# Two fetched tiles a block, copies as products with ones, and row stores on SyncE

## The chip, the cores and the metric

The kernel runs on one core of a Trainium2 chip. The metric is device time in microseconds (us), the median of three runs; the profile comes from one further execution. TensorE (PE in the profile, PEld for its weight loads), VectorE (DVE), ScalarE (ACT) and GpSimd (POOL) compute; SyncE (SP) issues transfers.

## The reference

A graph of 10000 nodes with 160000 random directed edges is propagated seven times, and a small attention runs over each node's eight states:

```python
h = x                                   # (10000, 128)
toks = [x]
for _ in range(7):
    msg = h[src] * deg_inv_sqrt[src, None] * deg_inv_sqrt[dst, None]
    h = segment_sum(msg, dst, N)        # one hop
    toks.append(h)
tok = stack(toks, axis=1)               # (N, 8, 128)
t = layernorm(tok)
attn = softmax((t @ wq) @ (t @ wk).T / sqrt(128))
o = tok + (attn @ (t @ wv)) @ wo
alpha = softmax(layernorm(o) @ w_r)
out = sum(alpha * o)                    # over the 8 tokens
```

## The kernel before

**Tables and slots.** The nodes lie in 79 tiles of 128. A hop keeps its input as a table in SBUF, `tab` (128 partitions, 79 tiles, 256 columns of f16: a high half and a low half of each value), and as rows in DRAM: `tabd` holds all tiles, `tabh` only the last ones. A *block* is the work for one tile of 128 destination nodes, some 2000 edges. Its edges are sorted by source into cells of 32 places (`CAP`). Four cells, for four source tiles, make one *slot tile* of 128 places. `NG` = 18 slot tiles cover the first 72 source tiles and are *gathered* from SBUF by TensorE: for each cell a matmul of 128 rows by 32 columns picks up to 32 rows of a source tile (line 578), four of them side by side fill one slot tile in PSUM. The 7 source tiles that remain are cut into 4 cells that make up `NI` = 1 slot tile, which is *fetched* from `tabh` by an indirect DMA that POOL issues (`fetch`, line 524). Edges beyond 32 in a cell go to one more tile, fetched from `tabd` (the index `i == NI`, matrix `Sov`). `NJ` = `NG` + `NI` is 19.

**A block** (`block`). Nine calls of `gather` fill nine PSUM banks in turn (ring of six), each with two slot tiles; each bank is copied to an f16 buffer `eb` of a ring (line 581; 14 buffers in hops 2 to 7), five of the nine by ACT and four by DVE (`evac`: ACT for 0, 2, 4, 5, 7). Then `begin` multiplies the fetched tiles into the accumulator (line 540), and `scat` multiplies each buffer by its 128 x 128 matrix of zeros and ones into it (line 554). The scatter of the last two buffers of a block is kept back (`lag` = 2) and runs behind the next block's gather. `close` sums the two halves (DVE, line 569).

**Behind it** stands `fin`: `entries` writes the next hop's table tile (ACT line 610, then DVE lines 611 and 612), `rows` stores it to DRAM (line 159, and line 163 for the tiles that `tabh` holds) and `token_out` scales the sum on POOL (line 619) and stores it as a token (line 621, SP). The last hop has `token_out` alone.

**Fetches.** `ahead` issues the fetches for the block two further on; the first of them is preceded by a copy of one column on POOL (line 523) that reads the block's first gather buffer, so that the fetch isn't issued too early. Fetches from `tabd` carry no such copy. Fetch tiles have three buffers. At a hop's start the overflow tiles of blocks 0 and 1 (`ogl`) can only be fetched when the last rows of the hop before have landed; line 567 uses them at these blocks' end.

**Stages.** Pass A and `decode` sort the edges. Hop 1 also makes the matrices of each block (`place`, `matrices`; lines 509 and 512 write them on DVE) and stores them in `GSd`. Hops 2 to 7 load them back (line 746, on SP, five buffers) and run the blocks in the order of tiles `4 * NG` to 78, then 0 to `4 * NG - 1`. The attention stage follows. The order on each engine comes from a scheduler that follows the order of the program where it can; every engine works its own list in order. Transfers that SP, ACT or POOL issue stand in that engine's list and wait there for their data.

Of the kernel before, what the change touches and what calls it, by code (L numbers as in the profile page):

```python
# [7 lines left out]
F32 = mybir.dt.float32  # L8
# [5 lines left out]
ALU = mybir.AluOpType  # L14
# [3 lines left out]

N, E, D, K = 10000, 160000, 128, 7
NT = 79  # L20
NG = 18
NI = 1
CELL = 334
NK = 79
NR = 10240
NCOL = E // 128
# [2 lines left out]
CAP = 32  # L29
NJ = NG + NI  # L30
NS = 4 * NJ
# [8 lines left out]
class Hops:  # L40
    def __init__(self, ctx, dp, missing, tab, tc, x, src, dst, dis):
# [31 lines left out]
                V.tensor_scalar(self.triw[:, w, :], ci, rf, None, op0=ALU.is_gt)  # L73
        self.ones32 = cp.tile([1, 128], F32, name="ones32")
        V.memset(self.ones32, 1.0)
        self.ones16 = cp.tile([128, 1], F16, name="ones16")
        V.memset(self.ones16, 1.0)
        self.iof = cp.tile([128, 128], F32, name="iof")
# [449 lines left out]
    def block(self, t, w, tab, og, pend, lag, runs, first, evac, fin, lead=False, late=False, mid=None, ahead=None,  # L528
              after=None):

        nc, V, A, T, G = self.nc, self.nc.vector, self.nc.scalar, self.nc.tensor, self.nc.gpsimd
        m = 257 if first else 256
        acc = []


        def fetched(i, start=False, stop=False):
            W = w[:, (NG + i) * 128:(NG + i + 1) * 128] if i < NI else self.Sov[:, t, :]
            T.matmul(acc[0][:, :256], W, og[i], start=start, stop=stop)  # L540
            if first:
                T.matmul(acc[0][:, 256:257], W, self.ones16, start=False, stop=False)

        def begin():
            acc.append(self.pacc.tile([128, 512], F32, name="acc", tag="acc"))
            for i in range(NI if late else NI + 1):
                fetched(i, start=i == 0)

        def scat(e, jj):
            if not acc:  # L550
                acc.append(self.pacc.tile([128, 512], F32, name="acc", tag="acc"))
            for j in range(e.shape[1]):
                J = 2 * jj + j
                T.matmul(acc[0][:, :m], w[:, J * 128:(J + 1) * 128], e[:, j, :m], start=first and J == 0,  # L554
                         stop=J == NG - 1 and not (first or late))
                if first and J == 0 and not lead:
                    for i in range(NI):
                        fetched(i)

        def close():  # L560
            if first:
                if lead:
                    for i in range(NI):
                        fetched(i)
                T.matmul(acc[0][:, 256:257], self.Sov[:, t, :], self.ones16, start=False, stop=False)
            if first or late:
                T.matmul(acc[0][:, :256], self.Sov[:, t, :], og[NI], start=False, stop=True)  # L567
            s = self.fp.tile([128, 128], F32, name="s")
            V.tensor_reduce(s, acc[0][:, 0:256].rearrange("p (h d) -> p d h", h=2), axis=X, op=ALU.add)  # L569
            fin(t, s, acc[0])  # L570

        def gather(jj):
            n = min(2, NG - 2 * jj)
            p = self.pg.tile([128, 2, 2, 128], F32, name="p")
            for j in range(n):
                for q in range(4):
                    s = 4 * (2 * jj + j) + q
                    T.matmul(p[32 * q:32 * q + 32, j], w[:, NJ * 128 + s * CAP:NJ * 128 + (s + 1) * CAP], tab[:, s, :], start=True, stop=True)  # L578
            e = self.ebuf[self.eb_i % len(self.ebuf)]
            self.eb_i += 1  # L580
            (A.copy if evac(jj) else V.tensor_copy)(e[:, :n, 0:256], p[:, :n].rearrange("p j h d -> p j (h d)"))  # L581
            pend.append(lambda: scat(e[:, :n], jj))

        jj = 0
        for i, n in enumerate(runs):
            for _ in range(n):
                gather(jj)
                if jj == 0 and not first and not mid:
                    ahead(self.ebuf[(self.eb_i - 1) % len(self.ebuf)][:, 0, 0:1])
                jj += 1  # L590
            if mid:
                mid(0)
            if not first:
                begin()
                if mid:
                    ahead()
            while len(pend) > lag:
                pend.pop(0)()
            if mid:
                mid(1)  # L600
            if after:
                after()
            if i == len(runs) - 1:
                pend.append(close)
            yield
# [17 lines left out]
    def run(self, ctx, att, nhop=K):  # L623
# [68 lines left out]
        with ExitStack() as c:  # L692
            self.gsp = c.enter_context(tc.tile_pool(name="gs2", bufs=5))
            self.pg = c.enter_context(tc.tile_pool(name="pg2", bufs=6, space=PSUM))
            self.pacc = c.enter_context(tc.tile_pool(name="pc2", bufs=2, space=PSUM))
            self.ogp = c.enter_context(tc.tile_pool(name="og2", bufs=3))
            self.fp = c.enter_context(tc.tile_pool(name="fp2", bufs=4))
            self.sp = c.enter_context(tc.tile_pool(name="sp2", bufs=2))
            self.more_ebufs(c.enter_context(tc.tile_pool(name="eb2", bufs=1)), 9, False)
            pend = []  # L700
            for k in range(2, nhop + 1):
                i = 1 - k % 2
                tab, din = self.tab[i], (self.tabd[i], self.tabh[i])
                ct = self.ctok[i]
                last = k == nhop
                V.tensor_scalar(ct, self.disT, self.sinv, None, op0=ALU.mult)


                def scale(part, n, i=i, k=k):
                    if part == 0 and n == 0 and k == 2:  # L710
                        self.count()
                    if part != 1 - n:
                        return
                    if n == 0:
                        mc = self.sp.tile([128, 1], F32, name="mc")
                        V.tensor_reduce(mc, self.mx[i], axis=X, op=ALU.max)
                        scale.m = self.colmax(self.pg, self.sp, mc, "p")
                        V.tensor_mul(scale.m, scale.m, self.rho)
                    else:
                        q = self.pow2_of(self.pg, self.sp, scale.m, 2.0 ** 8, "p")  # L720
                        V.tensor_mul(self.sinv, self.sinv, q[:, 1:2])
                        V.tensor_scalar(self.c1[i], self.dis2, q[:, 0:1], None, op0=ALU.mult)

                def fin(t, s, acc, k=k, ct=ct, last=last, i=i):
                    if not last:
                        self.entries(t, s, i)
                        self.rows(1 - i, self.tab[1 - i], t, t + 1, nc.scalar)
                    self.token_out(k, t, s, ct)


                order = [*range(4 * NG, NT), *range(4 * NG)]
                og = [[None] * (NI + 1) for _ in order]


                def ahead(n, after=None, og=og, order=order, din=din):
                    if n + 2 < NT:
                        for j in range(NI):
                            og[n + 2][j] = self.fetch(order[n + 2], j, din, after=None if j else after)
                    for m in range(0 if n == 0 else n + 2, min(n + 3, NT) if n >= 0 else 0):
                        og[m][NI] = self.fetch(order[m], NI, din, "ogl" if m < 2 else None)  # L740

                ahead(-2)
                ahead(-1)
                for n, t in enumerate(order):
                    w = self.gsp.tile([128, (NJ + NG) * 128], F8, name="w")
                    nc.sync.dma_start(w, self.GSd[t])
                    if k == 2 and n == 20:
                        att.constants(c, self.pg.tile([128, 512], F32, name="aw", tag="p"), self.ident)
                    if last and 40 <= n < 40 + 8 * FIRST:
                        att.load((n - 40) // 8, (n % 8,))  # L750

                    after = pend.pop() if n == 1 else None
                    for _ in self.block(t, w, tab, og[n], pend, 2, (9,), False, lambda jj: jj in (0, 2, 4, 5, 7), fin, n == 0, n < 2,
                                        (lambda part, n=n: scale(part, n)) if n < 2 and not last else None,
                                        lambda after=None, n=n: ahead(n, after), after):
                        pass
                while pend:
                    pend.pop(0)()
# [533 lines left out]
```

## Time and profile before

| | us |
|---|---|
| median of three runs (4150.82 to 4153.82) | 4152.88 |
| span of the profiled execution, first to last instruction | 4139.7 |
| TensorE busy | 3818.7 |
| VectorE busy | 3355.8 |
| ScalarE busy | 2692.1 |
| GpSimd busy | 1769.2 |

Busy time is that of the span; issuing a transfer and waiting for a semaphore count as idle. Hop 1 lies at about 410 to 1190 us, hops 2 to 7 from there to 3459, the attention stage behind. A row of the timeline gives start, duration, engine, line, operation, output and inputs, the number of instructions merged into it, and in brackets the idle time of the engine just before and what ended it. ACTq and SPq are the instructions of the queue that issue transfers.

### The profile page before, as it was taken

The page shows a single profiled execution, that of the slowest core. Times are in us where ns is not written, and L with a number is a line of the kernel's source. Part 1 is how long each engine was busy: PE and PEld are TensorE (multiplying, and loading weights), DVE is VectorE, ACT ScalarE, POOL GpSimd, SP SyncE. Part 2 cuts the span into 40 slices and gives each one's busy share as a digit, 9 for nine tenths or more (in the row PEclk, how much of TensorE's full clock was granted, in tenths as well). Part 3 has the DMA queues.
Part 4 walks back from the last instruction along what each step waited for, and adds up shares of the span by engine and source line. Part 5 has one row for each costly group of instructions (what it writes and reads, how often), then busy time and mean ns, then how long its engine had stood idle before and what let it go on. Part 6 is the DMA issues. An engine that isn't in the chain of part 4 may idle for free. (4 is left out here: it accounts for less than half of the span.)

```text
span 4139.7 us, 164058 instructions
## 1 busy us (share of the span) xinstructions
PE 3818.7 (92%) x69690; PEld 3021.9 (73%) x69690; DVE 3355.8 (81%) x6960; ACT 2692.1 (65%) x6830; POOL 1769.2 (43%) x2342
## 2 busy tenths in 40 slices
PE   5886889999989999999999999999999999999997
PEld 4665666666657777777777777777777887788785
DVE  8998999999967777777677777777775665999998
ACT  6883456666656665666566566656665657888885
POOL 0000333343345555555555555555555663222222
PEclk8998999999999999999999999999999999999998
DMA  3000444554556665665566656656666653222220
GB/s 109 23 2 17 143 148 153 152 157 150 158 163 185 186 184 180 185 185 184 179 184 186 181 183 186 186 176 186 187 185 191 188 184 105 75 72 81 72 77 17
DMA packets 321181, 594.87 MB, mean 144 GB/s; under 512 B 56183, under 2 KB 214101, under 8 KB 315189
## 3 DMA queue, kind: packets, MB, share of 16 engines
q1 hardware_dynamic: 220565, 478.42, 37.0%
q0 software_dynamic: 35392, 72.55, 6.4%
q10 hardware_dynamic: 64480, 33.33, 2.8%
q8 instruction: 546, 8.95, 0.9%
q14 instruction: 198, 1.62, 0.1%
HBM read 455.43 MB, written 128.67 MB: 141 GB/s over the span
## 5 line engine op out<-in xcount | busy, mean ns | idle before, releaser
L581 ACT CAST eb<-p 128x512 f16<-128x512 f32 x3065 | 1591.8, 600 | 670.9 <-PE p L578 575.6
L581 DVE CAST eb<-p 128x512 f16<-128x512 f32 x1912 | 1263.9, 688 | 439.1 <-PE acc L554 271.6
L578 PE MATMUL p<-tab,w 128*32 128x256 f16 x39816 | 1371.3, 275 | 105.0 <-ACT eb L581 38.1
L578 PEld LDWEIGHTS <-w 128*32 128x32 fp8e4 x39816 | 999.0, 96 | 406.7 <-issue 349.4
L554 PE MATMUL acc<-eb,w 128*128 128x256 f16 (+1 forms) x9954 | 1247.3, 274 | 9.2 <-ACT eb L581 2.3
L554 PEld LDWEIGHTS <-w 128*128 128x128 fp8e4 x9954 | 953.8, 98 | 172.7 <-issue 57.4
L524 POOL DMA_INDIRECT og<-tabh,oidx x553 | 616.6, 1115 | 769.2 <-DVE vi L476 389.0
L524 POOL DMA_INDIRECT og<-tabd,oidx x541 | 584.0, 1080 | 599.9 <-PE acc L554 262.7
L610 ACT ACTIVATE tab<-s,c 128x128 f16<-128x128 f32 x395 | 158.7, 402 | 359.7 <-DVE eb L581 262.9
L619 POOL TENSOR_SCALAR r<-s,ctok 128x128 f32<-128x128 f32 x474 | 295.7, 624 | 45.3 <-DVE s L569 28.2
L611 DVE SCALAR_TENSOR_TENSOR tab<-s,c,tab 128x128 f16<-128x128 f32 x395 | 139.0, 352 | 182.8 <-issue 166.5
L523 POOL COPY og<-eb 128x1 f16<-128x1 f16 x452 | 84.0, 186 | 422.7 <-ACT eb L581 422.7
L569 DVE TENSOR_REDUCE s<-acc 128x128 f32<-128x256 f32 x553 | 228.9, 414 | 23.1 <-PE acc L567 10.1
L991 ACT ACTIVATE junk<-tab 128x128 f32<-128x128 f32 x625 | 245.2, 394 | 0.0
L338 ACT ACTIVATE rs<-iof,rb 128x128 fp8e4<-128x128 f32 x784 | 231.9, 393 | 0.3
L512 DVE TENSOR_TENSOR w<-dsl,iof 128x2432 fp8e4<-128x2432 f16 x79 | 211.6, 2678 | 0.0
L977 PEld LDWEIGHTS po<-v,pT 128*128 128x128 f32 x1250 | 159.3, 193 | 43.6 <-issue 27.8
L966 PE MATMUL pv<-Wv,xT 128*128 128x131 f32 x1250 | 175.9, 283 | 2.5 <-ACT xT L946 1.5
L1049 POOL TENSOR_TENSOR p<-e,in 128x512 f32<-128x512 f32 (+1 forms) x40 | 40.8, 1021 | 320.7 <-DVE e L1047 320.7
L977 PE MATMUL po<-v,pT 128*128 128x128 f32 x1250 | 166.9, 277 | 7.0 <-DVE tab L983 5.4
L966 PEld LDWEIGHTS pv<-Wv,xT 128*128 128x128 f32 x1250 | 152.9, 191 | 19.3 <-issue 8.3
L540 PE MATMUL acc<-og,w 128*128 128x256 f16 x553 | 156.6, 283 | 0.0
(284 smaller groups left out, 4598.7 us busy)
## 6 DMA issues: line engine op xcount, KB each, us to landing
w<-gsd SPq DMA_DIRECT2D x474, 592.0 KB
gsd<-w SPq DMA_DIRECT2D x79, 592.0 KB
rb<-srow SPq DMA_DIRECT2D x79, 576.0 KB
tok<-r SPq DMA_DIRECT2D x546, 64.0 KB
tab<-tok SPq DMA_DIRECT2D x273, 128.0 KB
tabd<-tab ACTq DMA_DIRECT2D x395, 64.0 KB
og<-tabh,oidx POOLq DMA_INDIRECT x553
og<-tabd,oidx POOLq DMA_INDIRECT x541
```

The lines of the kernel that those rows point to most:

```text
L338: A.activation(ro[:, j - a, i, :], self.iof, AF.Abs_reciprocal_sqrt, scale=2.0 ** 21, bias=rb[:, j - VP, i:i + 1], saturate=False)
L512: V.tensor_tensor(w[:, :NJ * 128].rearrange("p (j d) -> p j d", d=128), dsl[:, g, :, None].to_broadcast([128, NJ, 128]), self.iof1[:, None ...
L524: self.nc.gpsimd.indirect_dma_start(out=o, out_offset=None, in_=src[0] if i == NI else src[1], in_offset=bass.IndirectOffsetOnAxis(ap=self ...
L554: T.matmul(acc[0][:, :m], w[:, J * 128:(J + 1) * 128], e[:, j, :m], start=first and J == 0, stop=J == NG - 1 and not (first or late))
L569: V.tensor_reduce(s, acc[0][:, 0:256].rearrange("p (h d) -> p d h", h=2), axis=X, op=ALU.add)
L578: T.matmul(p[32 * q:32 * q + 32, j], w[:, NJ * 128 + s * CAP:NJ * 128 + (s + 1) * CAP], tab[:, s, :], start=True, stop=True)
L581: (A.copy if evac(jj) else V.tensor_copy)(e[:, :n, 0:256], p[:, :n].rearrange("p j h d -> p j (h d)"))
L610: self.nc.scalar.activation(new[:, t, 0:128], s, AF.Copy, scale=c)
L619: self.nc.gpsimd.tensor_scalar(r, s, ct[:, t:t + 1], None, op0=ALU.mult)
L966: T.matmul(p[:, g - a, :], S[i]["xT"][:, g, :], Wv, start=True, stop=True)
L977: T.matmul(p[:, g - a, :], PT[i % 2][:, g, :], S[i]["v"][:, g, :128], start=True, stop=True)
L991: A.activation(j, S[i]["x"][:, g, :], AF.Square, bias=S[i]["x"][:, g, 0:1], scale=-1.0, accum_out=S[i]["sq"][:, g:g + 1])
```

## The change

`NG` becomes 17 and `NI` 2. The gather covers 68 source tiles; the remaining 11 are cut into 8 cells (`CELL` sets their width), which make two slot tiles, both fetched from `tabh`. `NJ` stays 19. The ninth call of `gather` then has one slot tile. Each block has two fetches from `tabh` and one from `tabd`; only the first carries the copy on POOL. `tabh` has 11 tiles, and a hop's order starts with those 11. DVE's copies of line 581 become products of the PSUM bank with a column of ones, broadcast over the bank. In hops 2 to 6 `rows` is issued by SP and not by ACT.

```diff
-NG = 18
-NI = 1
-CELL = 334
+NG = 17
+NI = 2
+CELL = 404
...
+        self.one = cp.tile([128, 1], F32, name="one")
+        V.memset(self.one, 1.0)
...
-            (A.copy if evac(jj) else V.tensor_copy)(e[:, :n, 0:256], p[:, :n].rearrange("p j h d -> p j (h d)"))
+            pv = p[:, :n].rearrange("p j h d -> p j (h d)")
+            if evac(jj):
+                A.copy(e[:, :n, 0:256], pv)
+            else:
+                V.tensor_tensor(e[:, :n, 0:256], pv, self.one[:, :, None].to_broadcast([128, n, 256]), op=ALU.mult)
...
-                        self.rows(1 - i, self.tab[1 - i], t, t + 1, nc.scalar)
+                        self.rows(1 - i, self.tab[1 - i], t, t + 1, nc.sync)
```

## The prediction

> **What bounds the kernel now.** I read four views in this order: busy time by stage, one block of a middle hop on each engine, the same block in the last hop, and the rows around a hop's start. First the stages (columns: busy us in 100 us with the number of instructions, granted clock, DMA share, GB/s).
>
> ```profile
> core 0: us, PE busy (x) PEld busy (x) DVE busy (x) ACT busy (x) POOL busy (x), PEclk, DMA share, GB/s
> 600.00:700.00 100.00, 91.48 (x1618) 67.48 (x1616) 98.01 (x136) 61.14 (x134) 38.09 (x22) 0.98 0.52 160
> 2400.00:2500.00 100.00, 97.18 (x1943) 77.97 (x1936) 74.59 (x148) 62.36 (x128) 58.84 (x85) 1.00 0.61 186
> 3200.00:3300.00 100.00, 100.00 (x2112) 84.92 (x2100) 66.88 (x115) 60.72 (x115) 63.43 (x92) 1.00 0.60 187
> ```
>
> The first row lies in hop 1: VectorE is at 98%. The second lies in hop 5, one of hops 2 to 6, the third in hop 7: TensorE is at 97 and 100% with the clock at 1.00. A block has 92 matmuls (72 of the gather, 2 of fetched tiles, 18 of the scatter), so 1943 in 100 us is 21 blocks, 2112 is 23. The same matmuls go 9% faster in hop 7, where no table entry is made. What hops 2 to 6 lose is seen in one block on PE, then on ACT:
>
> ```profile
> 2411.98 2.51 PE L578 MATMUL p<-tab,w 128*32 128x256 f16 x72
> ...
> 2414.66 2.13 PE L554 MATMUL acc<-eb,w 128*128 128x256 f16 x18
> 2416.72 1.49 PE L578 MATMUL p<-tab,w 128*32 128x256 f16 x48
> ```
>
> ```profile
> 2411.76 0.40 ACT L610 ACTIVATE tab<-s,c 128x128 f16<-128x128 f32 x1 [0.98 <-DVE eb L581]
> 2412.58 0.35 ACTq L159 DMA_DIRECT2D tabd<-tab  x1
> 2412.97 2.54 ACT L581 CAST eb<-p 128x512 f16<-128x512 f32 x5 [0.81 <-PE p L578]
> ```
>
> and the block of hop 7, PE and ACT:
>
> ```profile
> 3300.08 2.15 PE L578 MATMUL p<-tab,w 128*32 128x256 f16 x72
> ...
> 3304.45 2.15 PE L578 MATMUL p<-tab,w 128*32 128x256 f16 x72
> ```
>
> ```profile
> 3300.59 2.05 ACT L581 CAST eb<-p 128x512 f16<-128x512 f32 x4 [1.26 <-PE p L578]
> ```
>
> A block takes 2416.72 - 2411.98 = 4.74 us in hops 2 to 6 and 3304.45 - 3300.08 = 4.37 in hop 7. The gather itself takes 2.51 against 2.15. In hop 7 ACT empties the first PSUM bank 0.51 us after the gather began; in hop 5, 0.99 after (2412.97 - 2411.98). Between, ACT's own queue stands at the row store of line 159, which must wait for VectorE's half of the entry and then takes 0.35 to issue. After 48 matmuls all six gather banks are full and PE waits for that first copy. The view names "PE p" as releaser of ACT; its row of the queue shows the store.
>
> **Part 1, one slot tile fewer in the gather, one fetched tile more.** On PE this takes 4 gather matmuls (which run side by side) and one scatter matmul away and adds one fetched matmul: one step out of 38. A step is (2.13 - 0.27) / 17 = 0.11 us by the scatter row. So PE alone would need 4.37 - 0.11 = 4.26 us a block. On POOL it adds an indirect fetch per block, and POOL does them one at a time. A hop's start shows its pace with nothing to wait for, and a block behind it that of a fetch from the small table:
>
> ```profile
> 1966.22 0.94 POOL L524 DMA_INDIRECT og<-tabd,oidx  x1 [0.30 <-issue]
> 1967.47 0.95 POOL L524 DMA_INDIRECT og<-tabd,oidx  x1 [0.30 <-issue]
> 1968.72 0.95 POOL L524 DMA_INDIRECT og<-tabd,oidx  x1 [0.30 <-issue]
> 1969.70 0.62 POOL L619 TENSOR_SCALAR r<-s,ctok 128x128 f32<-128x128 f32 x1
> 1970.27 0.19 POOL L523 COPY og<-eb 128x1 f16<-128x1 f16 x1
> 1970.73 1.02 POOL L524 DMA_INDIRECT og<-tabh,oidx  x1 [0.27 <-issue]
> ...
> 1977.25 0.19 POOL L523 COPY og<-eb 128x1 f16<-128x1 f16 x1 [1.71 <-ACT eb L581]
> 1977.94 1.02 POOL L524 DMA_INDIRECT og<-tabh,oidx  x1 [0.51 <-POOL og L523]
> 1979.26 0.96 POOL L524 DMA_INDIRECT og<-tabd,oidx  x1 [0.30 <-PE acc L554]
> ```
>
> Start to start: copy to fetch 0.46, small-table fetch to the next fetch 1.32, big-table fetch to the token product 0.98, product to the next copy 0.57. POOL's turn without waits is 0.46 + 1.32 + 0.98 + 0.57 = 3.33 us now, far under 4.74. With a second small-table fetch it is 3.33 + 1.32 = 4.65 us. That is over PE's 4.26: the bound of hops 2 to 7 passes from PE to POOL, hidden as the fetches are today. POOL should then not wait at all: its copy needs ACT's first copy of the block, its fetches need fetched matmuls of earlier blocks, its product needs a sum of the block before, and PE is ahead in all of these. PE waits instead, for fetched tiles and, through the ring of 14 gather buffers (POOL's copy reads one of them, and it is written again in the next block), for POOL's copy. PE can get about one and a third blocks ahead, 5.5 us by estimate (4.26 plus the part of the next block up to the sixth buffer), before it is held; a hop keeps this head start once.
>
> The price of the added fetch is not shown in steady state. Below: spacing as between big-table fetches, 1.25 (1966.22 to 1967.47) for both small ones, so 4.65 - 0.14 = 4.51. Above: copy to fetch as at 1977.25, 0.69 instead of 0.46, so 4.88. I take 4.65, made of the rows nearest to a turn without waits. A gain below 4.26 is excluded, since PE stands there.
>
> **Part 2, rows stored by SP.** Both stores of `rows` leave ACT's queue. A block that also stores to the small table shows what an issue on ACT costs:
>
> ```profile
> 1989.98 1.49 PE L578 MATMUL p<-tab,w 128*32 128x256 f16 x48
> 1992.11 0.89 PE L578 MATMUL p<-tab,w 128*32 128x256 f16 x24 [0.64 <-ACT eb L581]
> ...
> 1995.21 1.49 PE L578 MATMUL p<-tab,w 128*32 128x256 f16 x48
> ```
>
> That block takes 1995.21 - 1989.98 = 5.23 us, 0.49 over 4.74 for one more store. So with the stores gone ACT starts as in hop 7 and PE's 4.26 holds in hops 2 to 6 too; the small table grows from 7 to 11 tiles, whose second store SP takes. The Trainium skill (DMA: Bandwidth & Descriptors, "Issuing engines are not separate DMA queues") says the issuing engine only matters for the time to initiate, usually small beside the transfer; the 0.49 us differ from that here, and by that rule blocks with two stores would stay at 5.23 - 0.11 = 5.12, eleven a hop over POOL's 4.65, and the sum would be 11 x 0.47 x 5 = 26 us smaller, 4128.
>
> On SP the stores stand behind the matrix load and the previous token store, which waits for POOL's product. With POOL a block late that delays rows and later matrix loads by about a block; five buffers hold the loads, and rows are read a hop later. Only the last rows of a hop are urgent. I price SP at 2 us a hop (0 to 4, by estimate: up to a block's wait at the hop's end). The transfers themselves (a matrix smaller by one tile of 37, one more fetch of 128 rows) fall on DMA engines that are at 0.61: 0.
>
> **Part 3, products with ones.** 4 of 9 PSUM copies in hops 2 to 7, and 16 in hop 1 (1912 - 4 x 474), become products with one PSUM and one broadcast SBUF operand; the ninth is half as large.
>
> ```profile
> L581 DVE CAST eb<-p 128x512 f16<-128x512 f32 x1912 | 1263.9, 688 | 439.1 <-PE acc L554 271.6
> L569 DVE TENSOR_REDUCE s<-acc 128x128 f32<-128x256 f32 x553 | 228.9, 414 | 23.1 <-PE acc L567 10.1
> ```
>
> ```profile
> L983 DVE TENSOR_TENSOR tab<-po,tab 128x512 f32<-128x512 f32 x156 | 102.6, 678 | 4.0 <-PE po L977 4.0
> L509 DVE TENSOR_SCALAR w<-rb,pid 128x2304 fp8e4<-128x2304 f16 x79 | 111.7, 1413 | 9.3 <-DMA rb<-srow 8.9 <-issue 0.4
> ```
>
> A two-operand form from PSUM took 678 ns where the copy took 688; the half one about 414. VectorE drops from 3.5 to 3.2 us a block, off the path: 0. In hop 1, which VectorE bounds, the row matrix of line 509 shrinks from 2304 to 2176 columns: 1413 x 128 / 2304 = 78 ns x 79 = 6 us less. POOL's third fetch fits there (38% busy).
>
> **The sum.** A hop's length now, first late fetch to first late fetch:
>
> ```profile
> 1963.70 0.94 POOL L524 DMA_INDIRECT ogl<-tabd,oidx  x1 [3.18 <-DMA tabd<-tab]
> ...
> 2345.31 0.95 POOL L524 DMA_INDIRECT ogl<-tabd,oidx  x1 [2.79 <-DMA tabd<-tab]
> ```
>
> 381.6 us. After: POOL's turns from the copy of block 3 to that of block 76, 73 x 4.65 = 339.5; from there to the fetched matmul of the last block 4.5 (0.46 and some 4 us until the tile is there, an estimate from the next rows); from that matmul to the copy of block 3 of the next hop as now:
>
> ```profile
> 1954.03 0.28 PE L540 MATMUL acc<-og,w 128*128 128x256 f16 x1
> ...
> 1968.44 0.27 PE L567 MATMUL acc<-ogl,Sov 128*128 128x256 f16 x1 [2.73 <-DMA ogl<-tabd,oidx]
> ```
>
> 1977.25 - 1954.03 = 23.2 (the fetch of 1963.70 is used at 1968.44, so 4.7 at the busiest place). With 2 for SP: 369.2, that is 12.4 less; five times (hops 2 to 6) -62. Hop 7: 79 x (4.65 - 4.37) = 22, less the head start of 5.5, +17. Hop 1: -6. Attention stage: 0. Sum -51. The profiled span is 4139.7 us, 13.2 below the median of 4152.9; I leave that difference as it is: 4139.7 - 51 + 13.2 = **4102 us**. Each 0.1 us on POOL's turn is worth 0.1 x (5 x 73 + 79) = 44 us, and the change is even at 4.65 + 51 / 444 = 4.765 us.
>
> **Rivals.**
> - *VectorE's products hold POOL up.* In hop 1 fetches are stretched by VectorE work on SBUF:
>
> ```profile
> 714.76 3.92 POOL L524 DMA_INDIRECT og<-tabd,oidx  x1 [5.30 <-PE acc L567]
> ```
>
> ```profile
> 717.15 1.42 DVE L509 TENSOR_SCALAR w<-rb,pid 128x2304 fp8e4<-128x2304 f16 x1
> ```
>
>  3.92 instead of 0.95. If the new products, three and a half of 0.68 us a block, do this, each turn grows by at least one of them: 5.33, so 444 x 0.68 = 302 more, 4404 us. It decides from 0.115 us a turn. Against it: those are 16-bit SBUF operations, and these read fp32 PSUM. The Trainium skill (GPSIMD Engine Reference, "1. Specifications") puts contention on 2-port modes or two SBUF inputs, which the product is not. Chance 0.18.
> - *Fetches cost POOL little.* If the spans are not occupancy, PE's 4.26 rules: 395 x (4.74 - 4.26) + 79 x 0.11 + 6 + 5 x 3.4 (the seven small-table blocks at 0.49) = 222 less, 3931 us. The Trainium skill (DMA: Bandwidth & Descriptors, "Anatomy of one DMA") calls descriptor generation small, with many descriptors before the cost shows. Against it stands the 1.25 us spacing with nothing to wait for. Chance 0.07.
>
> **How the numbers follow.** POOL's turn as bound has 0.75. Its ends, 4.51 and 4.88, give 4040 and 4204. The range is 4045 to 4205: it leaves out the rest of both rivals and little else. No change means within 0.2% (8 us, about what a measurement here can tell). Faster: turn under 4.745, 0.56 of the 0.75, and the second rival, together 0.63. Same: 0.08. Slower: 0.11 and the first rival, 0.29.
>
> **What would show it.** Right: POOL over 95% occupied from copy to copy at 4.65 us in hops 2 to 7, hops 6 and 7 at one pace, ACT's first copy 0.5 us behind the gather's start where PE isn't held, PE waiting on fetched tiles or full banks, products at 0.68. Wrong: fetches over 1.1 us in those hops, a POOL wait inside its turn, or blocks under 4.5 us.

## The result, and the profile after

The changed kernel took 4485.1 us (median of four runs, 4446.3 to 4511.0) against 4153.2 us of the kernel before: a ratio of 1.079, 95% interval 1.074 to 1.085. It is slower by 332 us; 4102 was forecast, and the range ended at 4205. The profiled execution is the fastest of the four, 4446.34 us with a span of 4444.5 us.

One stage of hop 5, as it was shown of before (busy us in 100 us with the number of instructions, granted clock, DMA share, GB/s), and the start of hops 4 and 5:

```profile
2400.00:2500.00 100.00, 84.77 (x1499) 62.60 (x1497) 54.85 (x131) 50.28 (x103) 62.25 (x81) 0.98 0.53 161
```

```profile
2034.87 0.94 POOL L526 DMA_INDIRECT ogl<-tabd,oidx  x1 [2.63 <-DMA tabd<-tab]
...
2472.82 0.94 POOL L526 DMA_INDIRECT ogl<-tabd,oidx  x1 [3.09 <-issue]
```

A block has 88 matmuls now (68, 3 and 17), so 1499 are 17 blocks where there were 21, at nearly the same clock; the hop takes 438.0 us and not 381.6 (hops 2 to 6 take 414.9 to 438.0, 426.4 on the mean, and 383.1 before). No engine is full: GpSimd is busy for 62 us of 100. The groups of the page that changed most (busy us, mean ns of one, idle time before them and what ended most of it):

```profile
L585 ACT CAST eb<-p 128x512 f16<-128x512 f32 x3065 | 1598.8, 591 | 1104.0 <-PE p L580 1047.6
L526 POOL DMA_INDIRECT og<-tabh,oidx x1106 | 1257.0, 1137 | 1117.8 <-DVE vi L478 387.6
L587 DVE TENSOR_TENSOR eb<-p,one 128x512 f16<-128x512 f32 x1912 | 1086.0, 618 | 905.4 <-PE p L580 854.9
L580 PEld LDWEIGHTS <-w 128*32 128x32 fp8e4 x37604 | 933.1, 96 | 786.6 <-issue 745.3
```

The work is not slower, the waiting is longer: ACT's copies stood idle 671 us before and 1104 now, VectorE's 439 and 905; the weight loads of TensorE's gather stood idle 407 us before and 787 now, 745 of them for nothing that the profile names ("issue"). Blocks come in two lengths (first fetched matmul of a block to that of the next): two in three blocks of hops 2 to 7 take 5.0 to 5.4 us, about 5.17, and one in five 5.6 to 6.0, about 5.8. The long ones are half of hop 7 and over a third of hops 4 and 5. First a short one, GpSimd from copy to copy:

```profile
2513.35 0.18 POOL L525 COPY og<-eb 128x1 f16<-128x1 f16 x1
2514.05 1.02 POOL L526 DMA_INDIRECT og<-tabh,oidx  x1 [0.51 <-POOL og L525]
2515.71 0.94 POOL L526 DMA_INDIRECT og<-tabh,oidx  x1 [0.65 <-PE acc L556]
...
2518.53 0.18 POOL L525 COPY og<-eb 128x1 f16<-128x1 f16 x1
```

Then a long one, on GpSimd, on ScalarE and on TensorE:

```profile
3503.59 0.18 POOL L525 COPY og<-eb 128x1 f16<-128x1 f16 x1 [0.92 <-ACT eb L585]
3504.28 1.02 POOL L526 DMA_INDIRECT og<-tabh,oidx  x1 [0.51 <-POOL og L525]
3505.61 0.94 POOL L526 DMA_INDIRECT og<-tabh,oidx  x1 [0.31 <-issue]
3506.86 0.94 POOL L526 DMA_INDIRECT og<-tabd,oidx  x1 [0.30 <-issue]
3507.82 0.63 POOL L625 TENSOR_SCALAR r<-s,ctok 128x128 f32<-128x128 f32 x1
3509.38 0.18 POOL L525 COPY og<-eb 128x1 f16<-128x1 f16 x1 [0.92 <-ACT eb L585]
```

```profile
3508.73 2.05 ACT L585 CAST eb<-p 128x512 f16<-128x512 f32 x4 [3.25 <-PE p L580]
```

```profile
3506.57 1.06 PE L580 MATMUL p<-tab,w 128*32 128x256 f16 x32
3508.59 1.55 PE L580 MATMUL p<-tab,w 128*32 128x256 f16 x36 [0.96 <-issue]
```

The gather begins at 3506.57 and has 32 matmuls behind it by 3507.63, four PSUM banks. ScalarE sees the first of them at 3508.73, over two microseconds after its matmuls began and 0.28 us after GpSimd's token product ended (3507.82 + 0.63). GpSimd then waits for that copy: it holds up what it waits for itself. So the turn is 0.69 + 1.33 + 1.25 + 0.96 + 0.63 + 0.92 = 5.8 us. In the short block GpSimd does not wait for the copy, but its second fetch starts 1.66 us after the first, not 1.33, and the row names TensorE as what it waited for.

TensorE stands for 0.96 us in the long block, and the profile calls that "issue". Its matmul of 3508.59 waits on ScalarE's semaphore (the counter by which an engine tells the others that it is done), and ScalarE's last copy of the block before had ended at 3505.48. The trace's semaphore events have no update of TensorE, VectorE or ScalarE between 3505.60 and 3508.65. So in this block it is not TensorE's news alone that came late.

The trace of before has the same mark, and it was not read. Its VectorE has four copies a block; the fourth came late:

```profile
2407.96 2.06 DVE L581 CAST eb<-p 128x512 f16<-128x512 f32 x3
...
2409.35 1.02 POOL L524 DMA_INDIRECT og<-tabh,oidx  x1 [0.27 <-POOL og L523]
...
2410.71 0.69 DVE L581 CAST eb<-p 128x512 f16<-128x512 f32 x1 [0.69 <-PE acc L554]
```

The last bank's matmuls were done by 2409.8, yet VectorE sat idle until 0.34 us after the end of GpSimd's fetch (2410.37). Counted over hops 2 to 7 by the trace's semaphore events (without the fetches of `ogl`): in the 1.3 us from a fetch's start TensorE's completions arrive 0.40 times a fetch in before (932 fetches) and then 2.26 times in the next 0.2 us. In the changed kernel it is 0.62 times (1402 fetches). The first fetch of a block shows it best: in before 5.0 of the matmuls that tell of their end do so, by their rows, in these 1.3 us, and 0.75 are heard. The burst has spacings down to 0.03 us, less than the 0.11 us of a matmul step, and the matmuls behind it are not late; so it is the news of the matmuls that is held, rather than the matmuls.

Not every fetch holds everything, and that tells the two lengths of block apart. In 315 of the 316 short turns of the changed kernel a completion of TensorE arrives during the third fetch, nearly always 0.8 to 0.9 us into it, and GpSimd's next copy doesn't wait. In 94 of the 96 long turns none arrives, and the copy waits. For ScalarE and VectorE the trace can't be counted like this: it has 4719 of ScalarE's 6110 updates and 4714 of VectorE's 5875, and some that it lacks were heard at once (ScalarE's half of an entry ends at 2506.22 with no update in the trace, and VectorE's half, which waits for it, begins at 2506.25).

### The profile page after: what moved, and what is told of

Its sections match the earlier page's. It is cut to its first block, busy times and chain, and to the rows that moved or that the text cites. A ratio compares the mean times of both kernels' runs of the same rounds, so it can differ in the third digit from the quotient of the medians.

```text
span 4444.5 us, 161925 instructions
## 1 busy us (share of the span) xinstructions
PE 3922.2 (88%) x67557; PEld 2960.6 (67%) x67557; DVE 3185.6 (72%) x6961; ACT 2700.8 (61%) x6830; POOL 2398.0 (54%) x2895
## 4 chain that ended last, share of the span: by engine, by line
PE 70%; DVE 15%; issue 6%; ACT 5%; DMA 2%; SPq 0%; another core or an unknown queue 0%; POOL 0%; POOLq 0%; DVEq 0%; ACTq 0%
PE p L580 28%; PE acc L556 21%; PE acc L542 5%; PE pv L972 3%; PE po L983 3%; DVE w L514 3%; PE pu L961 3%; ACT eb L585 2%; DVE o L212 2%; DVE ux L219 2%; PE pt L951 1%; PE tb L440 1%; ACT rs L340 1%; DVE oh L206 1%; DVE R L212 1%
## 5 line engine op out<-in xcount | busy, mean ns | idle before, releaser
L526 POOL DMA_INDIRECT og<-tabh,oidx x1106 | 1257.0, 1137 | 1117.8 <-DVE vi L478 387.6
L580 PE MATMUL p<-tab,w 128*32 128x256 f16 x37604 | 1467.2, 275 | 305.2 <-issue 258.9
L587 DVE TENSOR_TENSOR eb<-p,one 128x512 f16<-128x512 f32 x1912 | 1086.0, 618 | 905.4 <-PE p L580 854.9
L580 PEld LDWEIGHTS <-w 128*32 128x32 fp8e4 x37604 | 933.1, 96 | 786.6 <-issue 745.3
L556 PE MATMUL acc<-eb,w 128*128 128x256 f16 (+1 forms) x9401 | 1187.0, 274 | 7.8 <-DVE indeg L649 3.9
L556 PEld LDWEIGHTS <-w 128*128 128x128 fp8e4 x9401 | 901.5, 98 | 164.1 <-issue 52.3
L542 PE MATMUL acc<-og,w 128*128 128x256 f16 x1106 | 220.7, 279 | 0.0
L1071 POOL COPY pT<-t 32x512 f32<-32x512 f32 (+1 forms) x160 | 95.4, 596 | 120.7 <-DVE rx L1087 90.3
```

The lines of the kernel that those rows point to most:

```text
L526: self.nc.gpsimd.indirect_dma_start(out=o, out_offset=None, in_=src[0] if i == NI else src[1], in_offset=bass.IndirectOffsetOnAxis(ap=self ...
L587: V.tensor_tensor(e[:, :n, 0:256], pv, self.one[:, :, None].to_broadcast([128, n, 256]), op=ALU.mult)
```

## The experiments

Theory A after this look, put more strictly than these counts: TensorE's completions reach nobody while GpSimd works on an indirect fetch, and the third fetch lies over the start of the gather, where they are waited for. Rivals: the products on VectorE hurt GpSimd (B), SyncE's queue with the row stores is late (C), the added fetch's bytes or buffers are late, and not GpSimd (D).

**The parts alone.** `e1_tiles_only` is the changed kernel with the last two hunks undone; `e2_rows_only` and `e3_products_only` are the kernel before with one of them; `e4_third_fetch_direct` is the changed kernel with

```diff
                         for j in range(NI):
+                            if j:
+                                og[n + 2][j] = o = self.ogp.tile([128, 256], F16, name=f"og{j}")
+                                nc.sync.dma_start(o, din[1][0:128, :])
+                                continue
```

> The third fetch alone: 17 slot tiles gathered and two fetched, with plain copies on VectorE and the rows stored by ScalarE as before. Theory A (TensorE's completions reach nobody while GpSimd works on a fetch, and with three fetches in a turn one of these lies over the start of the gather): the loss is all here, 4450 to 4600 us, GpSimd's fetches still about 1.0 us and the gather's banks late. Theory B (the products on VectorE hold GpSimd's port or lengthen the turn): without products the block falls to GpSimd's plain turn of about 4.65 us and the time to 4150 or less. Theory C (SyncE's queue, now with the row stores in it, is what is late): 4100 to 4250 us.

> The rows stored by SyncE, nothing else changed. Theory A: the store's issue on ScalarE delayed the first copy of each gather, so a block of hops 2 to 6 comes down from 4.74 us to what hop 7, which stores no rows, shows (4.37 us): 5 x 79 x 0.37 = 146 us less, about 4005 us. Theory C (SyncE's queue is what hurts the changed kernel): 4153 us or slower, with SyncE's loads of w late.

> VectorE's copies as products with ones, nothing else changed. Theory A: 0.68 us for each product in place of the copy's duration, with VectorE not the bound: 4140 to 4180 us. Theory B (products and GpSimd's work hurt each other): slower by over 50 us.

> The changed kernel, but in hops 2 to 7 the second of the two fetched slot tiles is loaded by SyncE as a plain copy of 128 rows of the small table, not gathered by index on GpSimd: the same bytes into the same buffer at the same place of the program, TensorE's work unchanged, GpSimd's turn one fetch shorter. That part of the sum is left out (wrong rows are added). Theory A (GpSimd's third fetch, not its bytes, is the loss): block 4.3 to 4.45 us, 3980 to 4060 us. Rival D (the bytes, the buffer ring or TensorE's wait for the third tile are the loss): block stays near 5.2 us, 4400 us or more.

The four ran on another chip, and there the kernel before took 3949.6 us, not 4153. Measured: the tiles alone 4053.8 us, ratio 1.027 (1.025 to 1.028); the rows alone 3942.0, 0.998 (0.997 to 0.999); the products alone 3948.2, 1.000 (0.999 to 1.001); the third fetch by SyncE 3904.4, 0.990 (0.988 to 0.991), with a block of 4.26 us. The products alone change nothing, the stores gain a little, and the loss comes with the fetch and goes when SyncE copies as many bytes into the same buffer: on this chip B, C and D fall. But the tiles alone came out at 4054 and not over 4450, and SyncE's stores brought 8 us and not 146. Theory A as it stood was wrong about this chip.

**The whole change and the unchanged kernel on other chips.** `e5_whole_change` and `e9_before_itself` are the two kernels as they are.

> The whole change once more, next to the single parts. On the chip of the last four runs TensorE's completions arrive while GpSimd works on a fetch, and the kernel before takes 3950 us; on the chip of the first profiles they don't, and it takes 4153 us. Theory A (the third fetch makes GpSimd's turn 4.65 us everywhere, and a chip that holds the completions back pays half a microsecond more): where before takes about 3950 us, 4020 to 4070 us, a block of 4.65 us on the mean; where before takes about 4150 us, 4440 to 4510 us as first measured. Rival C (the three parts together hurt by themselves): 8% over the kernel before on either.

> The kernel before, unchanged, for its trace on the chip of these runs. Theory A (two kinds of chip): where it takes about 3950 us, its blocks are 4.37 us, TensorE's completions arrive while GpSimd is inside the first fetch of a block, and ScalarE's first copy begins about 0.45 us after the gather; where it takes about 4150 us, the completions come in a burst after the fetch and the block is 4.74 us as first profiled. Rival (the first profiles differ in something else than the completions): a block of 4.74 us with completions on time, or 4.37 us with a burst.

The whole change: 4067.6 us against 3947.9, ratio 1.030 (1.028 to 1.032). The kernel before: 3952.2 us, block 4.37. Its trace, same instructions, on ScalarE and TensorE and then on VectorE and GpSimd:

```profile
2442.70 0.40 ACT L610 ACTIVATE tab<-s,c 128x128 f16<-128x128 f32 x1 [0.49 <-DVE s L569]
2443.48 2.15 PE L578 MATMUL p<-tab,w 128*32 128x256 f16 x72
2443.65 0.35 ACTq L159 DMA_DIRECT2D tabd<-tab  x1
2444.04 2.54 ACT L581 CAST eb<-p 128x512 f16<-128x512 f32 x5 [0.94 <-PE p L578]
```

```profile
2444.22 2.48 DVE L581 CAST eb<-p 128x512 f16<-128x512 f32 x4 [0.41 <-PE p L578]
...
2445.15 1.02 POOL L524 DMA_INDIRECT og<-tabh,oidx  x1 [0.27 <-POOL og L523]
```

VectorE's four copies run without a gap across the same fetch of 1.02 us. TensorE's completions arrive 2.4 times in the 1.3 us from a fetch's start (932 fetches), where it was 0.40; in the changed kernel of the run before 3.2 (1402 fetches), where it was 0.62. Spacings of 0.04 us or less between them number 6 in hops 2 to 7 of this trace and 858 in the first one. Median durations are those of the first chip within 12 ns in every group of over 70 instructions but one (VectorE's half of the entry, 0.35 us there and 0.39 here); what differs is when completions arrive. With them on time, ScalarE's entry is done 0.38 us before the gather begins and the row store, 0.35 us of issue, ends 0.04 us before the first copy, which starts 0.56 us after the gather, where it was 0.99.

The changed kernel on the chip of its run, GpSimd over one turn, the group in which TensorE waits, and the start of two hops:

```profile
2442.51 0.19 POOL L525 COPY og<-eb 128x1 f16<-128x1 f16 x1
2442.97 1.02 POOL L526 DMA_INDIRECT og<-tabh,oidx  x1 [0.27 <-POOL og L525]
2444.29 0.95 POOL L526 DMA_INDIRECT og<-tabh,oidx  x1 [0.30 <-PE acc L556]
2445.55 0.95 POOL L526 DMA_INDIRECT og<-tabd,oidx  x1 [0.30 <-issue]
2446.54 0.62 POOL L625 TENSOR_SCALAR r<-s,ctok 128x128 f32<-128x128 f32 x1
2447.11 0.19 POOL L525 COPY og<-eb 128x1 f16<-128x1 f16 x1
```

```profile
L542 PE MATMUL acc<-og,w 128*128 128x256 f16 x1106 | 220.4, 279 | 130.6 <-DMA og<-tabh,oidx 127.4
```

```profile
2287.44 0.94 POOL L526 DMA_INDIRECT ogl<-tabd,oidx  x1 [5.14 <-issue]
...
2657.99 0.94 POOL L526 DMA_INDIRECT ogl<-tabd,oidx  x1 [5.02 <-DMA tabd<-tab]
```

This is the kernel that was forecast: GpSimd's turn without a wait, 0.46 + 1.32 + 1.26 + 0.99 + 0.57 = 4.60 us; TensorE waits for fetched tiles; a hop takes 370.6 us, where 369.2 was worked out. Over half of the blocks are 4.26 us, and longer ones, up to 6, stand between them, where TensorE waits for a tile; the mean is 4.6. But the kernel before needs 4.37 here, so it loses.

**Is it the turn, whatever fills it?** Two runs with the direct copy and, on GpSimd, two small products in the fetch's place; the second ties them to the tile:

```diff
# e6_plain_op_for_fetch
+                                nc.sync.dma_start(o, din[1][0:128, :])
+                                for _ in range(2):
+                                    nc.gpsimd.tensor_scalar(self.zz, self.zz, 1.0, None, op0=ALU.mult)
# e8_plain_op_tied
+                                for h in range(2):
+                                    nc.gpsimd.tensor_scalar(o[:, h * 128:(h + 1) * 128], self.zz, 1.0, None, op0=ALU.mult)
+                                nc.sync.dma_start(o, din[1][0:128, :])
```

> The third fetch by SyncE as a plain copy, as before, and in its place on GpSimd two products of 128x128 on a tile of its own, some 1.1 us together, which issue no transfer. (Wrong rows are added for the second fetched tile.) GpSimd's turn is then as long as with the fetch, about 4.5 us. Theory A on a chip that doesn't hold completions: the turn is the bound, whatever fills it, a block of about 4.5 us, 3960 to 4010 us where before takes 3950. On a chip that does: only fetches hold completions, so the same 4.5 us instead of 5.2, 4000 to 4060 us. Rival (GpSimd being busy with anything holds them): 5.1 us or more there.

> As the run with plain products in place of the third fetch, but the two products write the tile that SyncE's copy then fills, so that they keep the fetch's place in GpSimd's order. (Wrong rows are added for the second fetched tile.) GpSimd's turn is again about 4.6 us. Theory A, completions not held: the turn is the bound whatever fills it, 4.5 to 4.75 us a block on the mean, 4000 to 4090 us where before takes 3950. Rival (a fetch costs by its transfer, not by GpSimd's time): 4.26 us, 3905 us as with the plain copy alone.

The first missed its aim: 4287.3 us, ratio 1.086 (1.085 to 1.088). The products depended on nothing, and the scheduler put all 948 (746 ns each) before hop 2; hop 1 ended 380 us later and the hops ran at 4.26. It says nothing of the turn. The second, 3943.6 us, 0.999 (0.998 to 1.000), lies under the expected 4000 to 4090, because a product took 0.55 and not 0.6 us and follows the first fetch after 1.05 us, not 1.32: the median turn was 4.36 us, with no wait for ScalarE's copy in it. By theory A that is 0.10 over TensorE's 4.26, 474 x 0.10 = 47 us more than with the direct copy alone; against the kernel before the two differ by 0.94%, 37 us. The turn counts, not the transfer.

**A shorter turn.** `e7_token_on_scalar` is the whole change with one function shortened, `e10_before_token_scalar` the kernel before with the same, `e12_tiles_token` the tiles alone with it:

```diff
-        if k == 1:
-            self.nc.scalar.activation(r, s, AF.Copy, scale=ct[:, t:t + 1])
-        else:
-            self.nc.gpsimd.tensor_scalar(r, s, ct[:, t:t + 1], None, op0=ALU.mult)
+        self.nc.scalar.activation(r, s, AF.Copy, scale=ct[:, t:t + 1])
```

> The whole change, with the token product of hops 2 to 7 on ScalarE, not on GpSimd; nothing left out. GpSimd's turn loses 0.57 us and comes to about 4.1 us, under TensorE's 4.26. Theory A, no holding: TensorE bounds the block again at 4.26 to 4.35 us, 3905 to 3940 us where before takes 3950. With holding: shorter than the changed kernel by 0.3 to 0.6 us a block, 4200 to 4330 us where before takes 4150. Rival (the fetches' transfers are late, not GpSimd's turn): as the changed kernel.

> The kernel before with the token product of hops 2 to 7 on ScalarE. Theory A: GpSimd's turn is not its bound (3.3 us of 4.37), so the move alone brings nothing, 3935 to 3955 us where before takes 3950, and the gain of the changed kernel with this move comes from its 64 fewer passes a block. Rival (the move itself is the gain): 3900 us or less.

> The third fetch and the token product on ScalarE alone: plain copies, and the rows stored by ScalarE as in the kernel before. Theory A (only GpSimd's turn matters): 3900 to 3915 us where before takes 3950, so that products and SyncE's stores are not needed. Rival (with the token product in it too, ScalarE's queue delays its first copies): 3930 us or more.

The changed kernel with this move: 3903.1 us, 0.989 (0.987 to 0.991), faster than both kernels. The move in the kernel before: 3946.2, 1.000 (0.999 to 1.001), nothing. (A block has 88 matmuls and not 92, four fewer; for the expectation's 64 passes no trace has a count.) The tiles alone with it: 3909.9, 0.991 (0.989 to 0.993), 8 us over the full version on the same chip. The changed kernel with the move, its stage of hop 5 and one block:

```profile
2400.00:2500.00 100.00, 100.00 (x2050) 84.44 (x2052) 72.69 (x166) 75.83 (x165) 71.51 (x95) 1.00 0.72 216
```

```profile
2440.22 2.04 PE L580 MATMUL p<-tab,w 128*32 128x256 f16 x68
...
2444.48 2.04 PE L580 MATMUL p<-tab,w 128*32 128x256 f16 x68
```

TensorE is at 100% and a block is 4.26 us, its own floor.

**Looking for a chip that holds.** The direct copy and the version just shown went to further chips, the latter twice:

> The third fetch by SyncE as a plain copy, once more on another chip (wrong rows are added for the second fetched tile). Where before takes about 3950 us: 3905 us as measured. Where before takes about 4150 us and completions are held: theory A (held completions over the start of the gather are the extra loss) 4.3 to 4.75 us a block, 3950 to 4150 us; rival (something else of that chip) 5.2 us, 4440 us.

> The whole change with the token product on ScalarE once more, next to the same move in the kernel before. Where before takes about 3950 us: 3895 to 3915 us as measured. Where it takes about 4150 us: GpSimd's turn is shorter by 0.57 us, but two of its three fetches still lie over completions that are waited for: 4200 to 4330 us.

> The whole change with the token product on ScalarE, on another chip. Where before takes about 3950 us: 3895 to 3915 us. Where about 4150 us: 4200 to 4330 us by theory A, since three fetches still hold completions for about 3.8 us of a block.

The direct copy took 3898.7 us, 0.988 (0.987 to 0.990); the changed kernel with the move 3901.6, 0.988 (0.986 to 0.990), and 3901.9, 0.988 (0.987 to 0.990). On all four chips of these runs the kernel before took 3942 to 3953 us. The one that holds completions was not met again.

**The holding imitated.** So the wait was built in. GpSimd writes a one behind its token product, and the first copy of each gather is scaled by it, in the changed kernel (`e13_whole_gate`), with the token product on ScalarE (`e14_token_gate`) and in the kernel before (`e15_before_gate`):

```diff
 # token_out, behind the product
+            self.gate = self.fp.tile([128, 1], F32, name="gate", bufs=2)
+            self.nc.gpsimd.tensor_scalar(self.gate, s[:, 0:1], 0.0, 1.0, op0=ALU.mult, op1=ALU.add)
 # gather
-            if evac(jj):
+            if jj == 0 and self.gate is not None:
+                A.activation(e[:, :n, 0:256], p[:, :n].rearrange("p j h d -> p j (h d)"), AF.Copy, scale=self.gate)
+            elif evac(jj):
```

> The whole change, and the first PSUM copy of each gather (hops 2 to 7) is scaled by a one that GpSimd writes behind the token product of the turn before: as where completions held back by GpSimd's work reach ScalarE only when that work is done. Theory A: a circle closes, GpSimd's gate copy waits for ScalarE's first copy, and that for the end of GpSimd's turn: 4.65 + 0.2 for the new operation + 0.6 for the copy + some 0.25 for two semaphores = 5.7 us a block, 4500 to 4580 us. Rival (a late first copy is caught up elsewhere, and the holding is not what the first measurement paid for): 4.65 to 4.9 us a block, under 4200 us.

> The same gate in the changed kernel with the token product on ScalarE. Theory A: the turn is 4.1 + 0.2, so 5.1 to 5.2 us a block, 4300 to 4350 us: where completions are held, the shorter turn would still lose against the kernel before. Rival: 4.3 us, 3900 to 3930 us.

> The same gate in the kernel before. Theory A: turn 3.33 + 0.2 + 0.85 = 4.4 us, about TensorE's own 4.37: 3950 to 4000 us, so the kernel before hardly minds what costs the changed one 500 us. Rival: any wait of ScalarE's first copy costs all alike, 4300 us or more.

The changed kernel with the gate took 4649.0 us, 1.178 (1.176 to 1.180), block 5.82; with the move as well 4361.2, 1.105 (1.104 to 1.107), block 5.20; the kernel before with the gate 4005.4, 1.015 (1.014 to 1.017), block 4.45 in hops 2 to 6. The circle in the first of them:

```profile
2441.48 0.94 POOL L527 DMA_INDIRECT og<-tabd,oidx  x1 [0.30 <-issue]
2442.46 0.62 POOL L628 TENSOR_SCALAR r<-s,ctok 128x128 f32<-128x128 f32 x1
2443.05 0.19 POOL L630 TENSOR_SCALAR gate<-s 128x1 f32<-128x1 f32 x1
2444.03 0.18 POOL L526 COPY og<-eb 128x1 f16<-128x1 f16 x1 [0.79 <-ACT eb L586]
```

```profile
2443.27 0.69 ACT L586 ACTIVATE eb<-p,gate 128x512 f16<-128x512 f32 x1 [2.65 <-POOL gate L630]
```

The gate ends at 2443.24, ScalarE's copy begins 0.03 us later, and GpSimd's next copy comes when it is done. The blocks of 5.8 us of the first measurement show the same chain without a gate: product, ScalarE's first copy 0.28 us later, GpSimd's copy. 4649 lies above the expected 4500 to 4580, since the block is 5.82 and not 5.7 (474 x 0.12 = 57 us): the first fetch follows its copy after 0.69 us here, and 0.46 was reckoned. Nearly all blocks are long here, where the first measurement had one in five. The kernel before pays 60 us (4005.4 less 3945.1) for a wait that costs the changed one some 580 (4649.0 less 4067.6).

## Why the prediction was wrong

**TensorE alone, 4.26 us a block: right.** With the third fetch off GpSimd, or the token product off it, the blocks are 4.26.

**GpSimd's turn, 4.65 us with a part of 1.32 for the added fetch: nearly right where nothing is held.** It was 4.60, since the second small-table fetch spaced 1.26, near the lower price given, 1.25. The Trainium skill (DMA: Bandwidth & Descriptors, "Anatomy of one DMA") calls descriptor generation small. Here a fetch keeps GpSimd for 1.26 us, start to start, and that decides; no run splits it into its parts. As a forecast of a hop, 369.2 us, it holds on the chip of the second run (370.0 on the mean of hops 2 to 6) and on another for the tiles alone (368.2).

**"POOL should then not wait at all", the step that failed.** It rested on TensorE being ahead of GpSimd's copy and of its fetches. On the first chip TensorE was ahead, but most of its completions were not heard while GpSimd fetched, and with three fetches GpSimd is fetching when the gather begins. So in the long blocks GpSimd waited 0.92 us for a copy that its own work delayed, and the turn was 5.8 us; in the blocks of 5.17 the second fetch waited for a completion of TensorE that the first fetch had covered. On the mean of hops 2 to 7 the turn was 5.38 us, and 4.64 on the chip of the second run. Of the 0.74 between them 0.25 is the wait for the copy, 0.27 that of the second fetch, and 0.22 the step from the copy to the first fetch, 0.69 us in place of 0.46. This last is the prediction's upper end, and it needs no holding: it also stands in the traces of chips that hold nothing (the runs with the gate, and with the token product on ScalarE). At the prediction's own 44 us per 0.1 us of turn, 5.38 less 4.65 is 320 us; the profiled execution is 344 over the forecast, the median 383.

**"A block that also stores to the small table shows what an issue on ACT costs": read from one trace as a property of the store.** The stores themselves cost 8 us in all on the chip of their run, where no copy of VectorE is late. On the first chip the late copy made the entry late, and the store, waiting for the entry, stood in front of ScalarE's first copy. That chain is read from the two traces; the stores alone were not run on the first chip. The Trainium skill's rule that another issuing engine saves only the time of the issue (DMA: Bandwidth & Descriptors, "Issuing engines are not separate DMA queues") agrees with the 8 us, and not with the 0.37 us a block of the first trace: there the store's wait for its entry came on top.

**Where the sign came from.** The even point of 4.765 us compared GpSimd's new turn with a block of 4.74. That block was itself held up; on the other chips it is 4.37 and a hop of the kernel before 350.6 us (the mean of hops 2 to 6 in its trace there). With the forecast's 369.2 and its 17 for hop 7 (hop 1 left out) that is 5 x 18.6 + 17 = 110 us lost. Measured there: 120. So the forecast had the sign wrong on these chips by its base alone, with GpSimd's turn nearly right.

**Rivals.** VectorE's products do not hold GpSimd up: fetches in hops 2 to 7 stay at 0.94 to 1.14 us, a product takes 0.68, and on a later chip the products alone change nothing. Fetches do cost GpSimd their full time. The rival that came true, a wait of GpSimd on work that waits for GpSimd, was not on the list. Hop 1 was put at -6; on the later chips it ends 2 us later.

**Open.** What holds the completions, and whether it belongs to the first chip or to its condition then. That taking the fetch away would help there was not tried, nor were the products and the stores run alone there, as no later run met such a chip; the imitation gives the price and the form of the loss, not its cause. Open too is why one completion gets through in most third fetches, and how far ScalarE's and VectorE's completions are held like TensorE's.

## What to carry to other kernels

Adding work to an engine that looks idle is safe only if nobody waits on something that passes through that engine's turn: follow the circle from its first wait through the engine that releases it and back, and sum it as a bound of its own. When a copy sits idle and its data has long been computed, ask who was busy in between before pricing anything else; here, as the traces read, a single late VectorE copy carried both the block's 4.74 us and the warning. If a GpSimd turn is just over the bound, move a small operation off it: 0.57 us moved to ScalarE turned 3% slower into 1% faster on one chip, and was 1% faster on two more, though by the imitation not on one that holds completions (5.20 against 4.45 us a block).

## What the runs showed of the hardware

In the two traces of the first chip most of TensorE's completions were held back during GpSimd's indirect fetches. In the kernel before they came in a burst from 0.3 us after the fetch's end (0.40 per fetch in the first 1.3 us, then 2.26 in 0.2 us); on four others they arrived throughout (2.4 in 1.3 us for the same kernel, 2.0 to 3.7 in the 17 traces of it and its variants). The same kernel took 4153 us on the one and about 3947 on the others, a 5% difference with instruction durations equal within 12 ns in all groups of over 70 but one, and nearly the same granted clock (0.976 and 0.978).

An indirect fetch of 128 rows kept GpSimd for 0.95 us, and the next fetch began 1.25 to 1.33 us after its start where nothing was waited for.
